# A fused attention, spectral-mixing and two-MLP kernel: folds, conversions and the loop's tail at other steps, batch 1's mixing on another engine

## The chip, the cores and the metric

The kernel runs on one core of a Trainium2 chip. The metric is the device time of one execution in microseconds (us); the time given for a kernel is the median of its runs. A core has TensorE (PE in the profile; PEld its weight loads), VectorE (DVE), ScalarE (ACT), GpSimd (POOL) and SyncE (SP, which here only starts DMA transfers). Each engine works through its own queue in order and waits there for what it needs from others.

## The reference

Three stages follow one another, in float32, for 2 batches of 768 tokens.

1. Clustered attention, 8 heads of dimension 64. Queries and keys are given to the nearest of 16 centroids (the largest product of normalised vectors); `scores = q k^T / 8`, and where the clusters of query and key differ, -1e9; softmax over the keys; times V. The heads side by side give x (768 x 512).
2. Mixing and MLP: `u = x + real(fft2(x))` over tokens and features; normalised over features; `u + relu(un @ w_ch1) @ w_ch2` with 2048 hidden features.
3. A second MLP with a gate: `h = relu(x @ w_in)` with 1024 hidden features, a convolution of width 3 over tokens, `(h * sigmoid(conv)) @ w_out`.

## The kernel before

Most products are made of three: each operand is split into a high part and a low part (what is left), and high x high, high x low and low x high are summed in PSUM (`pass3`, L84). So nearly every matrix is converted twice, by a copy with rounding (high) and by a subtraction (low).

**The attention loop** (L791) has one step for each of the 96 tiles of 128 queries (6 tiles for each of 16 heads), and its order is written out by hand under `manual_schedule`. Step n issues the first scores and the row maximum of tile n+8 (`score_max`, L552: four matmuls, then a VectorE reduction), the second scores of tile n with the maximum subtracted in the product (`score_exp`, L595: four matmuls, then `exp` on ScalarE), the high and low part of tile n-1's probabilities (`prob_hi`, L614, on ScalarE, for the last even tiles on VectorE; `prob_lo`, L623, on GpSimd, or on VectorE for the tiles in LO_ON_DVE), and the value products of tile n-3 (`attn_v`, L633: 18 matmuls; LAG is 3). First and second scores take turns in three PSUM slots with all else that `slot` gives out, so a slot comes free when the reduction or the `exp` of three slots ago is done. Tiles 89, 91, 93 and 95 (IN_PLACE) keep their probabilities in the PSUM slot until the low part is made.

All other work is hung on steps in lists: `pre` ahead of a step's own work, `mid` within it, `aft`, `post` and `fill` behind it, in this order (L663 to L762). For each pair of heads m this is its load, its cluster products (`prep_sims`, at step 12m-19, 24 matmuls), the one-hot masks, the split of queries and keys (`prep_hi`, `prep_lo`), and the scaling of V (`v_max`, `v_turn`, `v_step`). For batch 0 it is also the mixing (`mixing`, L95, with its plan at L702): `fold` adds and subtracts mirrored halves of x (GpSimd), "row" makes one row of an extra operand (three VectorE operations on one partition), "even" and "odd" combine the folds, `high_part` and `low_part` split them, and the products y, z, ab follow; then sums into U, and the normalisation (`norm`). Two weights of the first MLP are converted ahead, in four quarters at AHEAD_STEPS, and sent to memory until step 87.

**The first MLP** (L1014 to L1045) has 16 blocks of 128 hidden features for each batch. Here the tile framework's planner sets the order of each engine from the program's order and estimated times. Block f's up product (`mlp1_up`, L856: 24 matmuls, two results that ScalarE and VectorE turn into high and low parts) precedes block f-1's down product (`down`, L905: 18 matmuls). A weight arrives as 64-bit words; `load_w` (L312) loads one and turns it into float32 (`from64`: four VectorE operations, one on ScalarE), and `split_w` splits it. Batch 1's mixing runs beside batch 0's blocks as the generator `later` (L991), advanced twice in each down product; its folds, low parts and final adds are on GpSimd (`G` at L128, L146, L227, L235, L993).

Of the kernel before, what the change touches and what calls it, by code (L numbers as in the profile page):

```python
# [9 lines left out]
F16 = mybir.dt.float16  # L10
# [39 lines left out]
def tile_net(ctx, tc, qk, v, cen, w12, w34, conv, dft, odd, out):  # L50
# [44 lines left out]
    def mixing(b, bank, bank2, low, other):  # L95
# [50 lines left out]
        stage("odd0", -1, 0, G, "ov")(fold)  # L146
# [86 lines left out]
        def ab_mirror(j):  # L233
            xj = X[:, j + 3].rearrange("p (a n) -> p a n", a=2)[:, ::-1]
            G.tensor_add(xj, xj, d["m", j][:, N2 + 1:N2 + 515].rearrange("p (a n) -> p a n", n=257)[:, :, 0:256])  # L235
# [55 lines left out]
    wst, cvs, w32 = [], [], {}  # L291
# [20 lines left out]
    def load_w(k, f):  # L312
# [3 lines left out]
        for op in from64(w, raw):  # L316
            op()
# [27 lines left out]
    ws, hs, acc, xs, gps, wbp, ws_b = {}, {}, {}, {}, [], [], {}  # L345


    with ExitStack() as actx:
# [314 lines left out]
        for m in range(1, NH // 2):  # L663
            k = 12 * m - 24
            if m > 1:
                at(pre, k, load_raw, m)
                at(post, k + 5, prep_sims, m)
                at(fill, k + 6, prep_first, m)
                at(fill, k + 7, prep_pick, m)
                at(fill, k + 8, prep_hi, m, (0,))  # L670
                at(fill, k + 9, prep_lo, m, 0, G)
                at(fill, k + (9 if m < 7 else 8), prep_hi, m, (1,))
                at(mid, k + 11, prep_turn, m)
                at(fill, k + (10 if m < 7 else 9), prep_lo, m, 1, G)
            at(fill, k + 14, load_v, m)
            at(aft, k + 17, v_max, m)
            at(mid, k + 19, v_turn, m)
            for i in range(4):
                at(aft, k + 19, v_step, m, i)
            at(fill, k + 24, v_step, m, 4)  # L680
            at(fill, k + 25, v_step, m, 5)
# [7 lines left out]
        for h in range(NH):  # L689
# [4 lines left out]
            for i in range(3):  # L694
                at(fill, 6 * h + 8 + i, attn_out, h, i)

        def two(name):
# [3 lines left out]
        first = mixing(0, lambda name: slot(name)[:, 0], two, V, G)  # L701
        plan = (("even0", fill, 54), ("even1", fill, 55), ("row", aft, 57), ("even", fill, 58), ("evenH", aft, 59),  # L702
                ("evenL", fill, 59),
# [10 lines left out]
        for i, t in enumerate((0, 3, 1, 4, 2, 5)):  # L714
# [3 lines left out]
            at(aft, n + 2, scale, t)  # L718
# [40 lines left out]
        at(fill, 92, first_split, 0)  # L759
        at(fill, 93, first_split, 1)  # L760
        at(fill, 95, first_split, 2)
        at(fill, 97, first_split, 3)  # L762
# [28 lines left out]
        for n in range(-LEAD, 6 * NH + 10):  # L791
# [40 lines left out]
    identb = ident16.bitcast(BF16)  # L832
    V.tensor_copy(identb, ident)
# [22 lines left out]
    def mlp1_up(g, f):  # L856
        if (g, f) == (0, 0):
            h = hs[0, g, f] = [dp.tile([128, 780], F32R, tag=t, bufs=1, name=f"first{t}")[:, 0:S] for t in ("e0", "e1")]
            w = ws[0, g, f]
        else:  # L860
            if g:
# [267 lines left out]
```

## Time and profile before

| | |
|---|---|
| median of 3 runs | 701.85 us (699.71 to 702.35) |
| profiled execution, its own time | 702.69 us |
| its span, first to last instruction | 700.9 us |
| mean granted TensorE clock | 0.994 |
| TensorE busy | 667.3 us, 95% of the span |
| VectorE busy | 543.9 us, 78% |
| ScalarE busy | 410.8 us, 59% |
| GpSimd busy | 200.3 us, 29% |

All rows below come from the one profiled execution; times in them count from the start of its span. Idle time in brackets is that of the engine just ahead of the instruction, with what ended it. A group's row gives the name of the result, `<-`, and the names of the inputs.

### The profile page before, as it was taken

The numbers are of one execution on the slowest core, as the hardware profiler recorded it, in microseconds if no ns is written. First come the engines' busy times: TensorE is split into PE (matmuls) and PEld (weight loads), VectorE is DVE, ScalarE is ACT, GpSimd is POOL, SyncE is SP. The second block draws the span as 40 slices with busy tenths as digits, with TensorE's granted clock in tenths as the row PEclk, the third lists the DMA queues.
The fourth block names the chain that finished last, engine by engine and source line by source line (L and its number), as shares of the span: only waits on it lengthen the run. The fifth ranks groups of instructions, "written<-read, shape, count | busy, mean of one in ns | idle before, by whom it ended". The sixth has DMA issues, their size and how long they took to land.

```text
span 700.9 us, 12789 instructions
## 1 busy us (share of the span) xinstructions
PE 667.3 (95%) x5106; PEld 504.6 (72%) x5106; DVE 543.9 (78%) x873; ACT 410.8 (59%) x664; POOL 200.3 (29%) x168
## 2 busy tenths in 40 slices
PE   8799999998899997989999999999999999999997
PEld 6598988987799886869998998555555555555553
DVE  7777889898877997999469976997634399867662
ACT  3478869787458787536335654676534367555442
POOL 8156658568646945121041000000000000000000
PEclk9999999999899999999999999999999999999999
DMA  7747696773633413224203350243000000001002
GB/s 219 198 110 193 158 244 157 213 209 84 155 87 78 106 62 122 68 98 144 113 0 121 121 180 10 77 156 122 0 2 1 1 0 1 1 1 71 20 1 90
DMA packets 22087, 66.50 MB, mean 95 GB/s; under 512 B 4502, under 2 KB 7562, under 8 KB 19212
## 3 DMA queue, kind: packets, MB, share of 16 engines
q1 hardware_dynamic: 21020, 61.94, 31.0%
q0 software_dynamic: 1008, 3.75, 2.0%
q8 instruction: 40, 0.66, 0.4%
q14 instruction: 19, 0.16, 0.1%
HBM read 40.94 MB, written 5.77 MB: 67 GB/s over the span
## 4 chain that ended last, share of the span: by engine, by line
PE 72%; DVE 16%; DMA 4%; issue 2%; ACT 2%; POOL 2%; SPq 1%; DVEq 0%; ACTq 0%; POOLq 0%
PE acc L86 8%; PE acc L87 8%; PE acc L85 8%; PE up L85 5%; PE up L87 5%; PE up L86 5%; PE av L641 5%; PE s L566 3%; PE t L601 3%; PE s L568 3%; PE t L603 3%; DVE m L571 3%; PE sim L440 3%; PE u L85 2%; PE u L87 2%
## 5 line engine op out<-in xcount | busy, mean ns | idle before, releaser
L629 POOL TENSOR_TENSOR p<-p,p 128x768 f16<-128x768 f32 x62 | 107.5, 1735 | 85.7 <-ACT p L621 59.5
L571 DVE TENSOR_REDUCE m<-s 128x1 f32<-128x768 f32 x96 | 90.5, 947 | 13.8 <-PE s L568 6.5
L609 ACT ACTIVATE p<-t,cbias 128x768 f32<-128x768 f32 x92 | 82.8, 900 | 26.2 <-PE t L603 25.0
L621 ACT CAST p<-p 128x768 f16<-128x768 f32 x88 | 73.0, 830 | 1.2
L641 PE MATMUL av<-V,p 128*128 128x65 f16 x1728 | 70.8, 195 | 2.8 <-POOL p L629 2.8
L641 PEld LDWEIGHTS <-p 128*128 128x128 f16 x1728 | 59.3, 99 | 18.3 <-issue 15.1
L601 PE MATMUL t<-X 128*128 128x384 f32 x192 | 54.5, 365 | 8.6 <-DVE m L571 6.9
L566 PE MATMUL s<-X 128*128 128x384 f32 x192 | 56.2, 374 | 3.2 <-DMA X<-ohd 1.8
L568 PE MATMUL s<-Y 96*128 96x384 f32 x192 | 50.0, 341 | 1.1 <-DMA Y<-G 1.1
L603 PE MATMUL t<-Y 98*128 98x384 f32 x192 | 50.2, 343 | 0.0
L85 PE MATMUL up<-un,wha 128*128 128x384 f32 x120 | 41.3, 344 | 2.7 <-DVE YcL L163 1.3
L85 PE MATMUL u<-x,wb 128*128 128x384 f16 x128 | 41.7, 326 | 1.3 <-DVE h L892 0.9
L87 PE MATMUL up<-un,wla 128*128 128x384 f32 x120 | 40.5, 338 | 1.8 <-DVE wla L853 1.8
L601 PEld LDWEIGHTS t<-X 128*128 128x128 f32 x192 | 32.0, 192 | 13.9 <-issue 6.7
L85 PE MATMUL up<-un,wa 128*128 128x384 f16 x128 | 41.7, 326 | 0.0
L87 PE MATMUL up<-un,wa 128*128 128x384 f16 x128 | 41.7, 326 | 0.0
L86 PE MATMUL up<-un,wa 128*128 128x384 f16 x128 | 41.7, 326 | 0.0
L87 PE MATMUL u<-x,wb 128*128 128x384 f16 x128 | 41.7, 326 | 0.0
L86 PE MATMUL u<-x,wb 128*128 128x384 f16 x128 | 41.7, 326 | 0.0
L86 PE MATMUL up<-un,wha 128*128 128x384 f32 x120 | 40.5, 338 | 0.0
L629 DVE TENSOR_TENSOR p<-p,p 128x768 f16<-128x768 f32 x30 | 37.7, 1257 | 0.1
L85 PE MATMUL acc<-wb,gH 128*128 128x512 f16 x96 | 36.4, 379 | 0.5 <-ACT gH L900 0.5
(368 smaller groups left out, 1701.0 us busy)
## 6 DMA issues: line engine op xcount, KB each, us to landing
rawa<-w SPq DMA_DIRECT2D x14, 1024.0 KB
rawb<-w SPq DMA_DIRECT2D x8, 1024.0 KB
raw<-qk SPq DMA_DIRECT2D x7, 768.0 KB
X<-G SPq DMA_DIRECT2D x14, 384.0 KB
Y<-G SPq DMA_DIRECT2D x14, 384.0 KB
vraw<-v SPq DMA_DIRECT2D x8, 384.0 KB
out<-y SPq DMA_DIRECT2D x12, 256.0 KB
X<-G SPq DMA_DIRECT2D x14, 192.0 KB
```

Of the source, the lines that this page charges most:

```text
L85: T.matmul(o, sH, mH, start=start, stop=False)
L86: T.matmul(o, sH, mL, start=False, stop=False)
L87: T.matmul(o, sL, mH, start=False, stop=stop)
L566: T.matmul(t[:, c, 0:384], X[:, 0, sl], X[:, 1, 384 * c:384 * c + 384], start=True, stop=False)
L568: T.matmul(t[:, c, 0:384], Y[0:96, 0, sl], Y[0:96, 1, 384 * c:384 * c + 384], start=False, stop=True)
L571: V.tensor_reduce(m6s[h][:, i:i + 1], t[:, :, 0:384], AX.XY, ALU.max, negate=True)
L601: T.matmul(t[:, c, 0:384], X[:, 1, sl], X[:, 0, 384 * c:384 * c + 384], start=True, stop=False)
L603: T.matmul(t[:, c, 0:384], Y[0:98, 1, sl], Y[0:98, 0, 384 * c:384 * c + 384], start=False, stop=True)
L609: A.activation(p, t[:, :, 0:384], AF.Exp, bias=cbias, scale=0.125)
L621: A.copy(p16[:, 0], p32s[n])
L629: eng.tensor_sub(p16[:, 1], p, p16[:, 0])
L641: T.matmul(o, p16[:, k, 128 * j:128 * j + 128], v16[:, i, h % 2, 65 * part:65 * part + 65], start=(i + j + k + part == 0), stop=(i == 5), ...
```

## The change

- The two even folds of batch 0 go from steps 54 and 55 to 52 and 53. "row" is now computed from one fold alone, as -2 times its first row, in one ScalarE operation (aft of step 60 instead of 57) and one VectorE operation ("rowL", fill of step 60); the constant it is multiplied with is changed to match.
- `prep_first` of pair 6 goes to VectorE, both `prep_lo` of pair 7 too. V's steps for pairs 6 and 7 come earlier; the four small ones of the other pairs are spread over four steps. The last quarter of the weights converted ahead goes from steps 53 to 62 to steps 65 to 68. LO_ON_DVE names other tiles from 54 on: 12 instead of 13 up to tile 87, and 91 and 94.
- From tile 88 the value products lag four steps, with five buffers instead of four; the loop has one step more. Tile 91 is not converted in place, and tile 88's high part is made by ScalarE.
- Weight 0 is split earlier, weight 1 is split within the loop (`second_split`), and block 0's up product is issued in steps 96 and 97 (`first_up`). The squares of weights 0 and 1 go behind blocks 13 and 14.
- In the first MLP `load_w` splits the weight at once, its operations stay behind those of the load before it (`issue_after`), and from block 4 on weight f+2 instead of f+3 is loaded behind block f. The scales come one block later. Batch 1's mixing uses VectorE instead of GpSimd throughout.
- The bf16 identity is made on GpSimd at step 84 instead of VectorE.

```diff
-             | {n for n in range(54, 87) if n % 12 in (1, 2, 7, 11)} | {87})
+             | {54, 56, 59, 61, 62, 67, 73, 77, 80, 83, 86, 87, 91, 94})
-AHEAD_STEPS = [12 * q + n for q in range(1, 5) for n in (5, 5, 5, 12, 14)]
-IN_PLACE = range(89, 96, 2)
+AHEAD_STEPS = [12 * q + n for q in range(1, 4) for n in (5, 5, 5, 12, 14)] + [65, 65, 65, 67, 68]
+IN_PLACE = (89, 93, 95)
...
-        stage("even0", 1, 0, G, "ev")(fold)
+        stage("even0", 1, 0, rest, "ev")(fold)
...
-            r1 = dp.tile([1, N2], F32, tag="row", bufs=1, name=f"r1{b}")
-            ev = d["ev", 0], d["ev", 1]
-            V.tensor_sub(r1[:, 0:257], ev[0][0:1, 0, 0:257], ev[1][0:1, 0, 0:257])
-            V.tensor_copy(Zx[0:1, 0:257], r1[:, 0:257])
-            V.tensor_sub(Zx[32:33, 0:257], r1[:, 0:257], f32(Zx[0:1, 0:257]))
+            A.activation(Zx[0:1, 0:257], d["ev", 1][0:1, 0, 0:257], AF.Copy, scale=-2.0)
+
+        @stage("rowL")
+        def _():
+            V.scalar_tensor_tensor(Zx[32:33, 0:257], d["ev", 1][0:1, 0, 0:257], -2.0, f32(Zx[0:1, 0:257]), ALU.mult,
+                                   ALU.subtract)
...
-            G.tensor_add(xj, xj, d["m", j][:, N2:N2 + 518].rearrange("p (a n) -> p a n", n=259)[:, :, 0:256])
+            rest.tensor_add(xj, xj, d["m", j][:, N2:N2 + 518].rearrange("p (a n) -> p a n", n=259)[:, :, 0:256])
...
+    A_LOADS = [(3,), (4,), (5,), ()] + [(f + 2,) for f in range(4, 14)] + [()] * 2
...
-        for op in from64(w, raw):
-            op()
+        with tc.issue_after(last_op[0]) if last_op else nullcontext():
+            for op in from64(w, raw):
+                i = op()
+            last_op[:] = [i.ins]
+        if k == "a":
+            ws[0, 0, f] = split_w(hp, 3, "a", f, f"a{f}", V)
...
-            p16 = probs[n] = ap.tile([128, 2, S], F16, tag="p16", bufs=4, name=f"p16_{n}")
+            p16 = probs[n] = ap.tile([128, 2, S], F16, tag="p16", bufs=5, name=f"p16_{n}")
-            elif n > 87:
+            elif n > 89 and n % 2 == 0:
...
+                at(fill, k + 6, prep_first, m, V if m == 6 else G)
+                at(fill, k + 9, prep_lo, m, 0, G if m < 7 else V)
...
+            n = {6: (62, 64, 66, 67, 68), 7: (68, 71, 72, 74, 74)}.get(m, (k + 14, k + 17, k + 19, k + 24, k + 25))
+            at(fill, n[0], load_v, m)
+            at(aft, n[1], v_max, m)
+            at(mid, n[2], v_turn, m)
             for i in range(4):
-                at(aft, k + 19, v_step, m, i)
+                at(aft, n[2] + (i if m < 6 else i // 2), v_step, m, i)
...
-        plan = (("even0", fill, 54), ("even1", fill, 55), ("row", aft, 57), ("even", fill, 58), ("evenH", aft, 59),
+        plan = (("even0", fill, 52), ("even1", fill, 53), ("row", aft, 60), ("even", fill, 58), ("rowL", fill, 60),
...
+        def first_up(i):
+            if i == 0:
+                hs[0, 0, 0] = [dp.tile([128, 780], F32R, tag=t, bufs=1, name=f"first{t}")[:, 0:S] for t in ("e0", "e1")]
+            h, tk = hs[0, 0, 0], slice(384 * i, 384 * i + 384)
+            o = slot(f"up0_{i}")[:, 0, 0:384]
+            up_half(o, ws[0, 0, 0], uns[0], i)
+            A.activation(h[0][:, tk], o, AF.Relu)
+            V.scalar_tensor_tensor(h[1][:, tk], o, 0.0, f32(h[0][:, tk]), ALU.max, ALU.subtract)
...
+        at(post, 96, second_split, 0)
+        at(post, 96, first_up, 0)
+        at(post, 97, second_split, 1)
+        at(post, 97, first_up, 1)
...
-            if 0 <= n - LAG < 6 * NH:
+            if 0 <= n - LAG < 88:
                 attn_v(n - LAG)
+            elif 88 <= n - LAG - 1 < 6 * NH:
+                attn_v(n - LAG - 1)
...
-        for name, f in mixing(1, up_bank, lambda name: (up_bank(name + "b"), up_bank(name + "a")), G, V).items():
+        for name, f in mixing(1, up_bank, lambda name: (up_bank(name + "b"), up_bank(name + "a")), V, V, V).items():
...
-            down(0, g, f, side, (1, 4) if g == 0 else (2,))
-            if g == 0 and f + 3 < 16:
-                load_w("a", f + 3)
+            down(0, g, f, side, (1, 4) if g == 0 and f else (2,))
+            for i in A_LOADS[f] if g == 0 else ():
+                load_w("a", i)
...
-            if (g, f) == (0, 13):
+            if (g, f) == (0, 14):
                 scales("a")
...
-    cs[0] = (k1[0] % 2 == 0)
+    cs[0] = 1.0
```

## Rows read from the trace of the kernel before

**Rows 1.** By stretch: start:end, length, busy PE PEld DVE ACT POOL, clock, DMA, GB/s.

```profile
164.00:186.20 22.20, 16.79 (x184) 14.70 (x182) 19.58 (x25) 13.87 (x21) 18.82 (x15) 0.85 0.33 71
186.20:262.00 75.80, 74.30 (x828) 68.38 (x825) 64.94 (x110) 55.48 (x81) 47.22 (x33) 1.00 0.38 95
262.00:280.30 18.30, 14.11 (x240) 12.34 (x240) 13.12 (x26) 13.54 (x23) 8.82 (x6) 1.00 0.31 117
280.30:312.50 32.20, 28.13 (x148) 25.30 (x145) 31.28 (x38) 15.40 (x29) 7.11 (x7) 1.00 0.19 66
312.50:440.00 127.50, 126.82 (x669) 113.44 (x668) 99.44 (x140) 63.39 (x120) 15.95 (x14) 1.00 0.30 106
```

**Rows 2.** The same table, the stretch behind the longest wait.

```profile
178.20:184.10 5.90, 5.90 (x48) 5.28 (x49) 4.64 (x6) 2.83 (x4) 4.26 (x4) 0.52 0.73 159
```

**Rows 3.** Timeline (start, length, engine, line), steps 57 to 61.

```profile
169.29 0.94 DVE L571 TENSOR_REDUCE m<-s 128x1 f32<-128x768 f32 x1
...
171.37 1.85 DVE L135 TENSOR_TENSOR r<-ev,ev 1x257 f32<-1x257 f32 x1 [1.13 <-POOL ev L115]
...
175.06 1.74 DVE L137 TENSOR_TENSOR Zx<-r,Zx 1x257 fp32r<-1x257 f32 x1
...
178.18 0.98 PE L601 MATMUL t<-X 128*128 128x384 f32 x2 [5.34 <-DVE m L571]
...
184.91 0.52 PE L601 MATMUL t<-X 128*128 128x384 f32 x2
...
186.19 0.42 PE L85 MATMUL y<-DC,EH 128*128 128x386 f32 x1
```

**Rows 4.** Tile Zx: VectorE's operations, duration in ns (shortest/median/longest).

```profile
L136 DVE CAST Zx<-r x2: 283/1030/1776, 173.3 to 297.6; 1x257 fp32r<-1x257 f32 x2
L137 DVE TENSOR_TENSOR Zx<-r,Zx x2: 418/1080/1743, 175.1 to 298.8; 1x257 fp32r<-1x257 f32 x2
```

**Rows 5.** Timeline, PE's waits in the loop's tail.

```profile
268.74 0.67 PE L641 MATMUL av<-V,p 128*128 128x65 f16 x16 [1.23 <-POOL p L629]
...
272.68 0.58 PE L601 MATMUL t<-X 128*128 128x384 f32 x2 [1.18 <-DVE d L649]
...
279.22 1.23 PE L641 MATMUL av<-V,p 128*128 128x65 f16 x34 [1.59 <-POOL p L629]
```

**Rows 6.** First MLP: timeline, groups (count, busy us, mean ns), one down product's ends.

```profile
303.32 2.39 DVE L300 SCALAR_TENSOR_TENSOR wa<-rawa,wa 128x1024 int32<-128x1024 int32 x1
...
306.91 0.45 PE L87 MATMUL up<-un,wla 128*128 128x384 f32 x1 [1.75 <-DVE wla L853]
...
L853 DVE TENSOR_TENSOR wla<-wa,wha 128x1024 fp32r<-128x1024 f32 x15 | 18.8, 1250 | 6.6 <-ACT wha L851 6.6
L300 DVE SCALAR_TENSOR_TENSOR wa<-rawa,wa 128x1024 int32<-128x1024 int32 x14 | 18.2, 1303 | 0.2
...
404.14 0.40 PE L85 MATMUL acc<-wha,hH 128*128 128x512 f32 x1
...
408.24 0.34 PE L85 MATMUL up<-un,wha 128*128 128x384 f32 x1
```

**Rows 7.** Prices: a group of the page, tiles and lines (ns), timeline.

```profile
L571 DVE TENSOR_REDUCE m<-s 128x1 f32<-128x768 f32 x96 | 90.5, 947 | 13.8 <-PE s L568 6.5
...
L629 POOL TENSOR_TENSOR p<-p,p x62: 1642/1657/2492, 29.5 to 277.4; 128x768 f16<-128x768 f32 x62
L629 DVE TENSOR_TENSOR p<-p,p x30: 935/952/1981, 33.2 to 263.3; 128x768 f16<-128x768 f32 x30
L497 DVE TENSOR_TENSOR G<-raw,G x1: 959/959/959, 6.9 to 6.9; 128x768 fp32r<-128x768 f32 x1
L206 ACT COPY a<-a384p x2: 365/365/365, 213.2 to 340.6; 1x258 f32<-1x258 f32 x2
...
176.93 0.24 DVE L578 TENSOR_TENSOR mr<-s,mr 6x128 fp32r<-6x128 f32 x1
177.96 0.59 DVE L654 SCALAR_TENSOR_TENSOR U<-av,vsc,d 128x384 f32<-128x384 f32 x1
```

More of the change, by code (lines that the diff above doesn't have):

```diff
@@ L1 @@
 import numpy as np
-from contextlib import ExitStack
+from contextlib import ExitStack, nullcontext
 import concourse.bass as bass
@@ L93, in tile_net, with mixing @@
     YcH, YcL = (dp.tile([128, 2, 512], F32R, name=n) for n in ("YcH", "YcL"))
-    def mixing(b, bank, bank2, low, other):
+    def mixing(b, bank, bank2, low, other, rest):
         X = U[:, 6 * b:6 * b + 6, :]
@@ L145, in mixing @@
         stage("evenL", "ev", 257, "E", low)(low_part)
-        stage("odd0", -1, 0, G, "ov")(fold)
+        stage("odd0", -1, 0, rest, "ov")(fold)
         stage("odd1", -1, 1, other, "ov")(fold)
@@ L234, in ab_mirror @@
             xj = X[:, j + 3].rearrange("p (a n) -> p a n", a=2)[:, ::-1]
-            G.tensor_add(xj, xj, d["m", j][:, N2 + 1:N2 + 515].rearrange("p (a n) -> p a n", n=257)[:, :, 0:256])
+            rest.tensor_add(xj, xj, d["m", j][:, N2 + 1:N2 + 515].rearrange("p (a n) -> p a n", n=257)[:, :, 0:256])
         for j in range(3):
@@ L699, in two @@
             return t[:, 0], t[:, 1]
-        first = mixing(0, lambda name: slot(name)[:, 0], two, V, G)
-        plan = (("even0", fill, 54), ("even1", fill, 55), ("row", aft, 57), ("even", fill, 58), ("evenH", aft, 59),
-                ("evenL", fill, 59),
+        first = mixing(0, lambda name: slot(name)[:, 0], two, V, G, G)
+        plan = (("even0", fill, 52), ("even1", fill, 53), ("row", aft, 60), ("even", fill, 58), ("rowL", fill, 60),
+                ("evenH", aft, 59), ("evenL", fill, 59),
                 ("odd0", fill, 60), ("y0", post, 61), ("odd1", fill, 61), ("y0L", pre, 62), ("y1", post, 62),
@@ L757, in first_split, with second_split @@
                 V.tensor_copy(w[i], src)
[L759 to L762, printed above, removed]
+        def first_up(i):
[6 more added lines that the diff above has]
+            V.scalar_tensor_tensor(h[1][:, tk], o, 0.0, f32(h[0][:, tk]), ALU.max, ALU.subtract)
+        def second_split(i):
+            w = [t.rearrange("p a n -> p (a n)") for t in (YcH, YcL)]
+            if i:
+                V.tensor_sub(w[1], w32["a", 1], f32(w[0]))
+                ws[0, 0, 1] = [t[:, 512 * j:512 * j + 512] for j in range(2) for t in w]
+            else:
+                A.copy(w[0], w32["a", 1])
+        at(fill, 84, G.tensor_copy, identb, ident)
+        at(fill, 91, first_split, 0)
+        at(fill, 92, first_split, 1)
+        at(fill, 93, first_split, 2)
+        at(fill, 94, first_split, 3)
+        at(post, 96, second_split, 0)
+        at(post, 96, first_up, 0)
+        at(post, 97, second_split, 1)
+        at(post, 97, first_up, 1)
         prep_hi(0)
@@ L790, in tile_net @@
         parts[2] = stack_parts(2)
-        for n in range(-LEAD, 6 * NH + 10):
+        for n in range(-LEAD, 6 * NH + 11):
             for f in pre.get(n, []):
@@ L856, in mlp1_up @@
     def mlp1_up(g, f):
[L857 to L867 removed]
+        if g:
+            t = hp.tile([128, S], F32R, tag="hH", bufs=3, name=f"h{g}_{f}").bitcast(F16)
+            h = hs[0, g, f] = [t[:, 0:S], t[:, S:2 * S]]
+            w = ws[0, g, f] = split_16(hp, "a", f) if f == 0 else ws[0, g, f]
+        else:
+            h = hs[0, g, f] = [hp.tile([128, S], F32R, tag=t, bufs=3, name=f"{t}{g}_{f}") for t in ("hH", "hL")]
+            w = ws[0, g, f]
         for i in range(2):
@@ L1014, in tile_net @@
     side = later()
-    mlp1_up(0, 0)
-    for f in range(2):
-        squares("a", f, cvs[0].tile([128, 2048], I32, tag="raw64", bufs=2, name=f"junk{f}")[:, 0:256].bitcast(BF16))
     load_w("a", 2)
@@ L1024, in tile_net @@
                 next(side, None)
-            down(0, g, f, side, (1, 4) if g == 0 else (2,))
-            if g == 0 and f + 3 < 16:
-                load_w("a", f + 3)
+            down(0, g, f, side, (1, 4) if g == 0 and f else (2,))
+            for i in A_LOADS[f] if g == 0 else ():
+                load_w("a", i)
+            if g == 0 and f in (13, 14):
+                raw = cvs[0].tile([128, 2048], I32, tag="raw64", bufs=2, name=f"junk{f}")
+                squares("a", f - 13, raw[:, 0:256].bitcast(BF16))
             if g == 1 and f in B_LOADS:
                 load_w("b", B_LOADS.index(f))
-            if (g, f) == (0, 13):
+            if (g, f) == (0, 14):
                 scales("a")
```

26 lines of the change are left out of this document (7 added, 19 removed).

## The prediction

> **What bounds the kernel now.** I began with a table of busy time by stretch, because every engine works on something different in each stage. TensorE is the bound nearly everywhere, so the question is where it stands still. Subtracting its busy time from the length of each stretch [rows 1] leaves 5.4 us in 164 to 186 us (steps 54 to 60 of the attention loop), 1.5 us in 186 to 262, 4.2 us in 262 to 280 (the tail of the loop, steps 88 to 98), 4.1 us in 280 to 312 (the first blocks of the first MLP), and 0.7 us from there to 440. What lies before 164 us and behind 440 us is hardly touched. In the first of these stretches the clock is a second loss: right behind the wait, 5.9 us run at a granted clock of 0.52, the lower of the two levels, 1.2 GHz [rows 2], in which 2.8 us of work are lost. So the first stretch can give 8.2 us, the four others 10.5 us.
>
> The timeline of the first stretch [rows 3] shows why. VectorE works on "row", three operations on one partition and 257 elements. Each takes 1.74 to 1.85 us, while GpSimd, busy 18.8 of 22.2 us [rows 1], is at work beside it. The row maximum of the next tile stands behind them in VectorE's queue; its scores hold a PSUM slot, and TensorE waits 5.34 us for it. The same operations in batch 1 [rows 4] take 0.283 and 0.418 us with GpSimd quiet: the work is some 1.1 us, the rest is waiting for GpSimd. The tail [rows 5] has three waits: 1.23 and 1.59 us for low parts of probabilities that come late from GpSimd, and 1.18 us that the list puts down to a small VectorE operation. There the slot of tile 91, which is converted in place in PSUM, is the likelier cause. In the MLP's first blocks [rows 6], TensorE waits 1.75 us for a weight's low part, which stood behind a 2.39 us weight conversion that normally takes 1.2 to 1.3.
>
> **Part by part.**
>
> *Folds and row.* The two even folds go from steps 54 and 55 to 52 and 53, where the cluster products (24 matmuls behind step 53) leave all other engines time. GpSimd finds a gap there, and its queue is then: low part 51, fold, low part 52, fold, low part 53. The first fold needs head 7's output, which precedes it in the same step. Low part 53 is due at step 56, with two of 1.66 [rows 7] and one fold ahead of it in the queue from step 53 on. The row's three VectorE operations become one on ScalarE (nearest row: 0.365 us for a copy of 258 elements on one partition) and one on VectorE (0.418 alone, 1.743 beside GpSimd [rows 4, 7]). Behind it in VectorE's queue now stands only step 61's maximum, and VectorE has slack from there, since the three y products (ten matmuls each) keep TensorE busy. The odd fold must wait for this operation, as both use one buffer; its first product is four steps away.
>
> What is late next is VectorE itself. From the maximum of tile 65 (start 169.3 [rows 3]; prep_first comes ahead of it, but low part 55 leaves, so I keep the start) to the end of that of tile 68, which releases the scores of step 61, it has four maxima of 0.95; low part 56, the even sum and its low part at 0.95 each (the last by the nearest row, 128x768, 0.959); one head output of 0.59; and seven small ones at 0.2 (nearest row 0.24) [rows 7]. This is 3.8 + 2.85 + 0.6 + 1.4 = 8.7 us. To it comes waiting for GpSimd. A low part on VectorE takes 0.952 in the median and 1.981 at worst [rows 7], so the three large ones add between 0 and 3.1; I take the middle, 1.5, because GpSimd, now busy 18.8 of 22.2 us [rows 1], is left with gaps. The end is 169.3 + 10.2 = 179.5, and the first y product 1.3 later, the distance from the scores of step 61 to it (184.91 to 186.19 [rows 3]): 180.8 instead of 186.2. That is a gain of 5.4 us; bounds: 3.8 with every wait, 8.2 with TensorE as the only limit. The slow clock is within it.
>
> Here a rule speaks against the change. Rows first: beside GpSimd the same operation is 1.3 to 1.5 us longer on VectorE, whatever its size [rows 4], and an operation that reads PSUM stays at 0.59 [rows 7]. The Trainium skill, "SBUF — State Buffer", section "SBUF: two separate sides", calls it an exclusive lock: a VectorE operation with two SBUF inputs and a GpSimd operation block each other for a whole instruction. By that rule each operation moved from GpSimd to VectorE exposes itself to such a wait, and the gain would be the lower bound, 3.8. The rows agree on the mechanism, and their median says that it does not hit each time.
>
> *The other operations at other steps.* The last quarter of the early weight conversion leaves steps 53, 60 and 62 for 65 to 68, four VectorE operations, with its load and store on SP's queue; the second cluster products and the first z product stand there. The last head pair's low parts (two of 0.959 alone, up to 2 beside GpSimd) go to VectorE at step 69, two fewer low parts of probabilities are on it later, and V's conversion for the last two pairs comes 5 to 11 steps earlier, with its load two or three steps ahead of its first use (three now). Cover: in 186 to 262 us VectorE is busy 64.9 of 75.8 [rows 1]. With this cover gone the price would be the two low parts, 2 us. V's conversion and two low parts leave steps 72 to 77, where the queue is full; I take a gain of 0.7 of the 1.5 us of waits, bounds -2 and 1.5. The spread of V's four small operations for the earlier pairs only splits a block: nothing, 0 to 0.5.
>
> *Tail.* From tile 88 the value products lag one step more, with a fifth buffer for probabilities; tile 91 leaves PSUM at once; low part 94 goes from GpSimd (1.66) to VectorE (0.95) [rows 7]; the squares of the first two weights leave ScalarE; and the first up product of the MLP (24 matmuls) is put between the last value products, so that it fills what waits are left. TensorE's work is unchanged. VectorE, busy 13.1 of 18.3 us there [rows 1], gets low part 94 (0.95), the second weight's low part (1.25 [rows 6]) and two low parts of the up product, and loses one high part: some 3 us more in a shorter time, which only just fits. Of 4.2 us I take 3.6, bounds 1.5 and 4.2.
>
> *First MLP.* Batch 1's folds, low parts and adds go to VectorE, ten operations, four of 0.96 [rows 7] and six shorter, under 10 us spread over 80, and its waits for GpSimd go: 1.2 us at the 2.39 row alone [rows 6]. The low part of a weight now precedes the next weight's conversion. But TensorE arrives 3.6 us earlier with the same conversions ahead, so the first blocks still wait for VectorE: of 4.1 us I take 1.5 as gained, bounds -3 and 4.1. The scales one block later: 0 to 4, taken as nothing, because the last down product is independent of them and covers their chain. The ones without a path (the bf16 identity on GpSimd, the constant's first row): 0.
>
> **Sum.** 5.4 + 0.7 + 3.6 + 1.5 = 11.2 us off the profiled execution's 702.69 (span 700.9, 1.8 around it): 691.5. That execution is 0.84 above the median of the three runs, 701.85, so carried to the median it is 690.6.
>
> **Rivals.**
> 1. *VectorE is the next wait in steps 54 to 60.* For it: it is busy 19.6 of 22.2 us there [rows 1], and it takes prep_first and low parts 54 and 56. Against it: 5.4 us of its busy time are the row. Then the first part gives 3.8 and the second -2: sum 3.8 - 2 + 3.6 + 1.5 = 6.9, time 695.
> 2. *The tail's gain is given back at once.* VectorE is busy 31.3 of 32.2 us in the first blocks [rows 1]; if TensorE only arrives earlier, the fourth part is -3 instead of 1.5: sum 5.4 + 0.7 + 3.6 - 3 = 6.7, time 695. Against it: the waits for GpSimd that go.
> 3. *Slower: each weight arrives too late.* From block 6 on a weight's load stands in the program directly ahead of its up product, one block later than now. If its conversion is not taken ahead, five operations of about 1.2 us [rows 6], 6 us, must fit under one down product of 4.1 us (404.14 to 408.24 [rows 6]): 1.9 us of wait in each of ten blocks, 19 us. The gains without the first blocks are 9.7, so the time is 711; it decides from five such blocks on. Against it: now the order is the program's only in part, and conversions start well before the down product ahead of them has ended.
> 4. *The change does not relieve GpSimd*, because the folds merely delay low parts 52 and 53: then TensorE waits at steps 55 and 56, and with tail and rest unchanged the gain is 3 us or less: 699.
>
> **How the numbers follow.** Forecast 0.64, rivals 1 and 2 0.13 and 0.13, rival 3 0.06, rival 4 0.04. A measurement of this kernel can tell about 0.5%, 3.5 us, from no change. The forecast and 0.22 of rivals 1 and 2 are faster than that (0.86), the 0.04 of them that goes worse and rival 4 lie within it (0.08), rival 3 beyond on the other side (0.06). The range: low with the first part at its ceiling and two more near theirs (8.2 + 1.2 + 4.2 + 4.0 = 17.6, off the median 701.85), 684; high with rivals 1 and 2 together (3.8 - 2 + 3.6 - 3 = 2.4, 699.5), cut to what leaves one in ten outside, 698.5.
>
> **What would show it.** In the changed profile TensorE's longest wait on a row maximum between steps 54 and 61 is under 2 us, the granted clock stays at 1.00 there (2.4 GHz), the two row operations take under 0.5 us on ScalarE and under 1.8 on VectorE, the wait for GpSimd's low parts in the tail is gone with up matmuls in its place, and the blocks behind have under 3 us of waits for VectorE. Wrong would be: waits for weight low parts block after block (rival 3), a wait for VectorE of 3 us or more in the first blocks (2), or a stall at half clock at steps 56 to 60 again (1, 4).

## The result, and the profile after

The changed kernel takes 692.25 us (median of 4 runs, 689.78 to 693.6); the kernel before, measured beside it, 701.89. The ratio is 0.9857 (95% interval 0.983 to 0.9883), a gain of 9.6 us; 690.6 was forecast. The profiled execution is the shortest of the four, 689.78 with a span of 688.0, so in its rows 12.9 us are gone.

The busy times of the page come first, then the table by stretch, which answers to [rows 1] and has its columns. The first stretch begins 1.7 us earlier than there, as the steps ahead of it do; the next two are cut at the first y product and at step 88; the tail now holds the first up product, so that it ends at the second weight's.

```profile
PE 664.9 (97%) x5106; PEld 503.0 (73%) x5106; DVE 546.1 (79%) x883; ACT 413.8 (60%) x667; POOL 179.9 (26%) x153
...
162.30:178.79 16.49, 14.81 (x183) 12.30 (x182) 15.23 (x21) 13.79 (x22) 11.91 (x8) 1.00 0.30 68
178.79:256.50 77.71, 74.82 (x830) 68.69 (x826) 69.37 (x114) 55.65 (x81) 48.46 (x35) 1.00 0.49 132
256.50:276.78 20.28, 18.31 (x268) 16.25 (x264) 18.58 (x30) 14.69 (x21) 7.28 (x5) 1.00 0.01 2
276.78:308.00 31.22, 31.22 (x160) 28.85 (x161) 30.91 (x44) 16.43 (x30) 0.00 (x0) 1.00 0.28 98
308.00:440.00 132.00, 131.68 (x703) 113.83 (x702) 106.15 (x167) 69.99 (x135) 7.11 (x7) 1.00 0.26 90
```

TensorE still bounds the kernel. Its idle time in steps 54 to 60 falls from 5.4 to 1.7 us and the clock there rises from 0.85 to 1.00 (2.4 GHz); in the first MLP's blocks it falls from 4.1 to nothing. In the long stretch between, it grows, from 1.5 to 2.9.

The same landmarks in both traces give where the 12.9 us lie. Up to step 53 the trace is 1.7 us shorter (the head of the kernel, not touched). From there to the first y product 5.7 are gained, from it to step 88 1.9 given back. The tail, up to where TensorE is free for the second weight's up product, gains 2.4. The first MLP up to the second MLP's first product gains 4.4; the 0.8 us that TensorE waited for VectorE ahead of the second weight's up product, before the change, are counted here. All behind it gains 0.6.

The timeline of steps 57 to 61, answering [rows 3]:

```profile
167.85 0.94 DVE L578 TENSOR_REDUCE m<-s 128x1 f32<-128x768 f32 x1
...
176.41 0.95 DVE L578 TENSOR_REDUCE m<-s 128x1 f32<-128x768 f32 x1
176.92 0.40 ACT L133 ACTIVATE Zx<-ev 1x257 fp32r<-1x257 f32 x1
...
177.42 0.62 PE L608 MATMUL t<-X 128*128 128x384 f32 x2 [0.19 <-DVE m L578]
...
178.00 2.52 POOL L118 TENSOR_TENSOR ov<-U 128x765 f32<-128x765 f32 x1
178.79 0.42 PE L85 MATMUL y<-DC,EH 128*128 128x386 f32 x1
178.85 1.96 DVE L137 SCALAR_TENSOR_TENSOR Zx<-ev,Zx 1x257 fp32r<-1x257 f32 x1
...
180.84 0.96 DVE L578 TENSOR_REDUCE m<-s 128x1 f32<-128x768 f32 x1
180.86 0.44 PE L155 MATMUL y<-OD,Zx 128*128 128x386 f32 x1 [0.23 <-DVE Zx L137]
...
181.85 0.62 PE L573 MATMUL s<-X 128*128 128x384 f32 x2 [0.55 <-DVE m L578]
```

From the maximum of tile 65 to the end of that of tile 68 VectorE takes 9.5 us (167.85 to 177.36), where 10.2 were predicted and 14.1 were taken before (169.29 to 183.38). The row's low part still meets a GpSimd fold and takes 1.96 us. Two waits of TensorE follow from it: 0.23 us of the last matmul of the first y product (L155), and 0.55 us of the next first scores, whose slot is held until the maximum behind the row's low part (180.84) is done.

Three of TensorE's waits from the list of waits (total, times, longest), and the timelines of the two longer ones:

```profile
PE t L608 <- DVE m L578: 1.9, 7, 0.4
...
PE unT L275 <- DVE p L634: 1.8, 1, 1.8
PE s L573 <- DVE m L223: 1.2, 1, 1.2
...
209.85 1.66 POOL L636 TENSOR_TENSOR p<-p,p 128x768 f16<-128x768 f32 x1 [6.06 <-ACT p L628]
209.99 2.35 DVE L506 TENSOR_TENSOR G<-raw,G 128x768 fp32r<-128x768 f32 x1
...
214.08 0.58 PE L573 MATMUL s<-X 128*128 128x384 f32 x2 [1.25 <-DVE m L223]
...
261.02 1.65 POOL L636 TENSOR_TENSOR p<-p,p 128x768 f16<-128x768 f32 x1
261.08 1.87 DVE L270 TENSOR_SCALAR y<-U,mv,rs 128x512 f32<-128x512 f32 x1
...
262.87 0.94 DVE L634 TENSOR_TENSOR p<-t,p 128x768 f16<-128x768 f32 x1
263.87 0.66 PE L275 MATMUL unT<-ident,y 128*128 128x128 f32 x4 [1.84 <-DVE p L634]
...
270.51 0.42 PE L85 MATMUL up<-un,firstEH 128*128 128x384 f32 x1
```

At step 69 a low part of pair 7, now on VectorE, is held by GpSimd and takes 2.35 us; the eviction of the mixing's products (L223), for which TensorE waits, stands behind it. The wait itself falls in step 71. In the tail the last normalisation of batch 0 is held in the same way (1.87 us; 0.54 where nothing holds it). The changed kernel issues it ahead of its step's own work instead of behind it, a move that the list of the change does not name. Tile 89's low part now stands behind it, and the transposed U waits for the slot of that tile. The up product (from 270.51) fills what waits followed.

### The profile page after: what moved, and what is told of

It is laid out like the page before. It is cut to its first block, busy times and chain, and to the rows that moved or that the text cites. A ratio compares the mean times of both kernels' runs of the same rounds, so it can differ in the third digit from the quotient of the medians.

```text
span 688.0 us, 12771 instructions
## 1 busy us (share of the span) xinstructions
PE 664.9 (97%) x5106; PEld 503.0 (73%) x5106; DVE 546.1 (79%) x883; ACT 413.8 (60%) x667; POOL 179.9 (26%) x153
## 4 chain that ended last, share of the span: by engine, by line
PE 68%; DVE 20%; ACT 3%; issue 3%; DMA 2%; POOL 1%; SPq 1%; DVEq 0%; POOLq 0%
PE acc L87 7%; PE acc L85 7%; PE acc L86 7%; PE up L85 5%; PE up L86 5%; PE up L87 5%; PE av L648 4%; PE s L573 3%; DVE m L578 3%; PE t L608 3%; PE s L575 3%; PE sim L447 3%; PE t L610 3%; PE u L85 2%; PE u L87 2%
## 5 line engine op out<-in xcount | busy, mean ns | idle before, releaser
L628 ACT CAST p<-p 128x768 f16<-128x768 f32 x90 | 74.7, 830 | 1.3
L636 DVE TENSOR_TENSOR p<-p,p 128x768 f16<-128x768 f32 x31 | 39.2, 1265 | 0.2
L85 PE MATMUL up<-un,wha 128*128 128x384 f32 x112 | 38.0, 339 | 0.0
L86 PE MATMUL up<-un,wha 128*128 128x384 f32 x112 | 37.8, 338 | 0.0
L87 PE MATMUL up<-un,wla 128*128 128x384 f32 x112 | 37.6, 337 | 0.0
```

The lines of the kernel that those rows point to most:

```text
L85: T.matmul(o, sH, mH, start=start, stop=False)
L86: T.matmul(o, sH, mL, start=False, stop=False)
L87: T.matmul(o, sL, mH, start=False, stop=stop)
L636: eng.tensor_sub(p16[:, 1], p, p16[:, 0])
```

## The experiments

Twelve kernels in three groups. Each group has its own runs of the kernel before: medians 703.32, 702.75 and 701.44 us for groups one to three; ratios are to these.

**Group one: the row alone.** The kernel before with

```diff
-            ("row", aft, 57), ("even", fill, 58)
+            ("row", aft, 60), ("even", fill, 58), ("rowL", fill, 60)
```

with the new "row" and "rowL" and the constant's first row.

> The kernel before with the row alone changed: one ScalarE operation in the aft list of step 60 and one VectorE operation in the fill list, with the constant's first row; the folds stay at steps 54 and 55. Theory (the stall is three VectorE operations that each wait for a GpSimd instruction): the 5.3 us wait of TensorE at step 59 and the half clock behind it go, the first y product comes 4 to 7 us earlier, and the time falls by 4 to 7 us, ratio 0.990 to 0.994. Rival (the stall is GpSimd's lateness, because the folds stand in its queue between the low parts): TensorE still waits 3 us or more between steps 55 and 61 and the ratio is above 0.996.

Measured: 701.7 us, ratio 0.9983 (0.9958 to 1.0008), no difference clear of the noise. Its table by stretch and one row of its timeline:

```profile
160.00:180.00 20.00, 16.22 (x195) 13.83 (x195) 17.14 (x23) 15.56 (x23) 20.00 (x16) 1.00 0.32 71
...
300.00:320.00 20.00, 16.63 (x74) 15.29 (x73) 17.23 (x20) 10.14 (x19) 1.89 (x2) 0.83 0.29 105
...
179.91 1.06 PE L642 MATMUL av<-V,p 128*128 128x65 f16 x16 [2.10 <-POOL p L630]
```

The wait for VectorE is gone; GpSimd is busy all of the 20 us, and TensorE waits for its low parts. Yet this trace is 4.3 us ahead of the one before at the first up product's eviction (278.39 against 282.68; 2.0 of them lie ahead of step 46, where the kernels are the same), and only 1.6 at the end. The rest is lost in the first MLP. TensorE's waits there add up to 4.0 us in both traces; what differs is the clock behind them, 0.83 between 300 and 320 us instead of 1.00.

**The folds alone.** The kernel before with

```diff
-            ("even0", fill, 54), ("even1", fill, 55)
+            ("even0", fill, 52), ("even1", fill, 53)
```

> The kernel before with the two even folds alone at steps 52 and 53; the row stays three VectorE operations at step 57. Theory: the row no longer waits for the fold (1.1 us), but its three operations still meet a busy GpSimd, so they take 1 to 1.8 us each, TensorE still waits 2 us or more for the row maximum, and the gain is 0 to 2.5 us, ratio 0.9965 to 1.000. Rival (GpSimd's lateness is the cause): the stall is gone, ratio 0.994 or less.

Measured: 700.84 us, ratio 0.9972 (0.9948 to 0.9996). The theory holds: the row's stall remains, the longest wait for a maximum is 2.9 us, and the gain of 2.5 us is at the upper end of its range.

**The changed kernel once more**, as the base of the others.

> The changed kernel as it is, once more, beside the partial ones. Median 691 to 693.5 us, ratio 0.983 to 0.988. If an execution with a mean granted clock near 0.995 is recorded, the stretch in which the clock is low should lie directly behind a wait of TensorE, and tell what the difference of some 3 us between its executions is.

Measured: 690.8 us (690.04 to 693.85), ratio 0.9834 (0.9794 to 0.9875). The profiled execution (692.44 us) has the same waits, but behind the one of 1.84 us its clock is 0.91 between 260 and 280 us.

**Batch 1's mixing back on GpSimd.** The changed kernel with

```diff
-        for name, f in mixing(1, up_bank, ..., V, V, V).items():
+        for name, f in mixing(1, up_bank, ..., G, V, G).items():
```

> The changed kernel with batch 1's first folds, low parts and final adds on GpSimd again (the other folds on VectorE, as before the change). Theory (the first blocks' waits came from VectorE operations held up by GpSimd): VectorE's conversions near the folds take over 2 us again and TensorE loses 1.5 to 3 us in the first blocks of the first MLP, 1.5 to 3 us slower than the changed kernel. Rival (the order of the conversions, with the low part ahead of the next weight, did it): TensorE has no wait in the first blocks and the time is within 1 us of the changed kernel.

Measured: 698.56 us, ratio 0.9944 (0.9922 to 0.9966): 7.8 us slower than the changed kernel, far more than either theory had. Timeline and table of its first blocks:

```profile
289.79 2.82 POOL L115 TENSOR_TENSOR ev<-U 128x765 f32<-128x765 f32 x1
290.83 1.80 DVE L113 TENSOR_TENSOR ev<-U 128x3 f32<-128x3 f32 x1
...
306.95 0.45 PE L85 MATMUL y<-DC,EH 128*128 128x386 f32 x1 [3.65 <-DVE hL L900]
...
300.00:320.00 20.00, 16.36 (x78) 14.89 (x77) 17.56 (x19) 10.47 (x19) 2.98 (x3) 0.91 0.33 114
```

A VectorE operation on three columns takes 1.80 us beside GpSimd's fold (0.15 in the changed kernel); a low part of the hidden features comes 3.65 us late, and the clock falls behind it.

**Group two: folds and row together**, in the kernel before (both diffs above).

> The kernel before with the two even folds at steps 52 and 53 and, together with it, the new row (one ScalarE operation and one VectorE operation at step 60); GpSimd's list of low parts, the tail and the first MLP stay as before. Folds alone gave 2.5 us and the row alone 1.6 us, each with a wait of 2 to 3 us left in steps 54 to 61. Theory (two limits stand side by side, VectorE's row and GpSimd's queue, and only both together free TensorE): the gain is more than the sum of the two, 5 to 8 us, about 696 us; no wait over 1.5 us between 160 and 185 us, the clock 1.00 there, and the first y product at about 179 to 181 us instead of 186.2. Rival (the relief of GpSimd from low parts 54, 56, 59 is needed as well): 3 to 4 us, 699 to 700 us, with a wait of 2 us or more for a low part of GpSimd left in steps 55 to 62.

Measured: 703.65 us, ratio 1.0018 (0.9994 to 1.0042). The theory of two limits falls, and so does the rival: there is no wait for GpSimd there. Timeline and table:

```profile
180.57 2.32 DVE L303 SCALAR_TENSOR_TENSOR ahead<-ahead 128x512 uint32<-128x512 uint32 x1
...
182.92 1.74 DVE L137 SCALAR_TENSOR_TENSOR Zx<-ev,Zx 1x257 fp32r<-1x257 f32 x1
...
184.72 0.44 PE L155 MATMUL y<-OD,Zx 128*128 128x386 f32 x1 [2.24 <-DVE Zx L137]
...
180.00:200.00 20.00, 17.21 (x162) 15.70 (x161) 17.10 (x21) 10.00 (x15) 8.51 (x6) 0.91 0.40 110
```

The first y product starts at 180.62, as forecast. Its last matmul waits 2.24 us for the row's low part, which stands in VectorE's queue behind a step of the early weight conversion (L303, step 60), itself held by GpSimd. The clock falls behind this wait.

**The mixing off GpSimd alone.** The kernel before with batch 1's `G, V` turned into VectorE throughout (folds and final adds through the new argument `rest`).

> The kernel before with one thing changed: batch 1's folds, low parts and final adds on VectorE instead of GpSimd. In the changed kernel putting them back on GpSimd cost 7.8 us. Theory (the gain of the first MLP is this move alone): TensorE's waits for VectorE behind 300 us shrink from 4.1 us to under 1.5, gain 3 to 5 us, 697 to 699 us. Rival (the move pays only together with the first up product in the loop and the weights' new order, because VectorE, 31.3 of 32.2 us busy there, has no room for ten more operations): 0 to 1.5 us, or slower by up to 3.

Measured: 697.53 us, ratio 0.9924 (0.9898 to 0.995), 5.2 us faster. The theory holds. Its first blocks, answering to the fourth line of [rows 1], and three groups of VectorE between 280 and 312 us, first before, then here:

```profile
280.00:312.00 32.00, 31.25 (x162) 28.72 (x161) 31.47 (x45) 16.52 (x30) 0.00 (x0) 1.00 0.27 99
...
L300 DVE SCALAR_TENSOR_TENSOR wa<-rawa,wa 128x1024 int32<-128x1024 int32 x4 | 6.0, 1510 | 0.0
L299 DVE TENSOR_SCALAR wa<-rawa 128x1024 int32<-128x1024 int32 x4 | 4.3, 1106 | 0.0
L115 DVE TENSOR_TENSOR ev<-U 128x765 f32<-128x765 f32 x1 | 2.6, 2612 | 0.0
...
L300 DVE SCALAR_TENSOR_TENSOR wa<-rawa,wa 128x1024 int32<-128x1024 int32 x4 | 4.9, 1215 | 0.0
L299 DVE TENSOR_SCALAR wa<-rawa 128x1024 int32<-128x1024 int32 x4 | 2.7, 684 | 0.0
L115 DVE TENSOR_TENSOR ev<-U 128x765 f32<-128x765 f32 x2 | 1.9, 954 | 0.0
```

VectorE is about as busy as before (30.8 us of these 32 then), with 45 operations instead of 37. The same operations are shorter now: by the three groups some 4.5 us of its busy time before were waiting for GpSimd (4 times 0.30, 4 times 0.42, and 1.66), and that is where the moved operations found room.

**The normalisation back in its place.** The changed kernel with

```diff
-            at(aft if t != 5 else pre, n + 2, scale, t)
+            at(aft, n + 2, scale, t)
```

> The changed kernel with the last normalisation of batch 0 (scale of tile 5) back behind low part 89 in VectorE's order, as before the change. Theory (its two VectorE operations stand ahead of tile 89's low part, one of them held 1.3 us by GpSimd, and so the slot of tile 89 in PSUM comes free 1.8 us late for the transposed U of the MLP): the wait of 1.84 us at that product falls under 0.8 us, and so does the half clock that stood behind it in one of two profiles; 1 to 2.5 us faster than the changed kernel, 689 to 690 us. Rival (the transposed U then waits for its normalised input instead, as scale comes later): within 0.5 us, 690.5 to 691.5 us, or slower.

Measured: 691.51 us, ratio 0.9835 (0.9811 to 0.9859): no difference, as the rival said. The transposed U waits 1.1 us for its normalised input instead of 1.8 for the slot.

**The first up product back at the MLP's start**, in the changed kernel:

```diff
-        at(post, 96, first_up, 0)
-        at(post, 97, first_up, 1)
...
+    mlp1_up(0, 0)
     load_w("a", 2)
```

> The changed kernel with the first up product (24 matmuls of the two halves, 2 evictions and 2 low parts) taken out of the tail and put back at the start of the MLP. Theory (in the tail it fills TensorE's waits, worth most of the 2.4 us that the tail gained): waits of 1 to 1.6 us for probabilities' low parts and the last value products return, 1.5 to 3 us slower than the changed kernel, 692.5 to 694 us. Rival (the waits went through the longer lag and low part 94 on VectorE, and the place of the up product does nothing): within 0.7 us of the changed kernel.

Measured: 694.81 us, ratio 0.989 (0.9869 to 0.9912), 3.3 us slower than the run above it and 4.0 slower than the changed kernel of group one: at least as much as the whole tail had gained hangs on this place; the longer lag without it shows no gain in this trace. The waits that the theory named do not come back, though: the longest two for low parts or value products there are 0.7 and 0.3 us. What it has beside the wait of 1.8 us for tile 89's slot is one of 1.1 us for VectorE at the second weight's up product, and a clock of 0.91 between 260 and 280 us.

**Group three: four parts together.** The kernel before with folds, row, batch 1's mixing on VectorE, and

```diff
-             | {n for n in range(54, 87) if n % 12 in (1, 2, 7, 11)} | {87})
+             | {54, 56, 59, 61, 62} | {n for n in range(63, 87) if n % 12 in (1, 2, 7, 11)} | {87})
```

> The kernel before with four parts of the change together: the even folds at steps 52 and 53, the new row, the low parts of tiles 54, 56, 59, 61 and 62 on VectorE (before: 55, 59, 61, 62; so GpSimd loses 54 and 56 and gets 55), and batch 1's mixing on VectorE. The last of these alone gave 5.2 us (697.5); row and folds together gave nothing by themselves, with 2.2 us of wait left for the row's low part and two of 1.6 for GpSimd. Theory (GpSimd's list of low parts was what still held steps 52 to 61, and what those steps give was given back in the first blocks of the MLP as long as batch 1's mixing was on GpSimd): now 4 to 5 us more than with the mixing alone, 692.5 to 694 us, no wait over 1.5 us in steps 54 to 61. Rival 1 (the weight conversion that stands at steps 60 and 62 takes the place of the wait): 1 to 2 us more than the mixing alone, 695.5 to 697 us. Rival 2 (the list of low parts does nothing): 697 to 698 us.

Measured: 697.98 us, ratio 0.994 (0.9916 to 0.9964). Rival 2: no more than the mixing alone. The wait at L155 is still there, 2.27 us, with the clock at 0.83 between 180 and 200 us.

**The same with the last weight conversion at steps 65 to 68:**

```diff
-AHEAD_STEPS = [12 * q + n for q in range(1, 5) for n in (5, 5, 5, 12, 14)]
+AHEAD_STEPS = [12 * q + n for q in range(1, 4) for n in (5, 5, 5, 12, 14)] + [65, 65, 65, 67, 68]
```

> The same as the run above it in this list, and besides that the last quarter of the early weight conversion at steps 65 to 68 instead of 53, 60 and 62, as in the changed kernel. Theory (steps 54 to 61 are free by then): within 0.7 us of the run above. Rival (VectorE's conversion at steps 60 and 62 is the next wait): 2 to 4 us faster than the run above, 691 to 693 us. What still differs from the changed kernel is then the tail, the first up product, the weights' order and V's parts; by the run with the up product put back these are worth 2 to 4 us in the changed kernel.

Measured: 693.92 us (690.87 to 699.09), ratio 0.9897 (0.9861 to 0.9932). The runs scatter, and the two intervals overlap by 0.0016; the medians are 4.1 us apart, close to the 2 to 4 of the rival. The trace is clearer: the row's low part is as long as ever, and the conversion no longer stands ahead of it.

```profile
180.89 1.94 DVE L137 SCALAR_TENSOR_TENSOR Zx<-ev,Zx 1x257 fp32r<-1x257 f32 x1
...
182.88 0.44 PE L155 MATMUL y<-OD,Zx 128*128 128x386 f32 x1 [0.19 <-DVE Zx L137]
```

The distances between three landmarks of each trace, in us, settle these steps. They start from the exponential of tile 46 (141.97 us in the trace before), so that what differs ahead of it drops out, and end with that of tile 62:

| kernel | tile 46 to first y | first y to tile 62 | sum |
|---|---|---|---|
| before | 44.2 | 3.5 | 47.7 |
| mixing off GpSimd (steps 46 to 62 unchanged) | 43.2 | 3.5 | 46.7 |
| row | 40.8 | 4.6 | 45.4 |
| folds | 43.3 | 3.5 | 46.8 |
| folds, row | 38.7 | 7.8 | 46.4 |
| folds, row, low parts, mixing | 39.4 | 8.1 | 47.4 |
| the same with the conversion moved | 38.6 | 4.7 | 43.3 |
| changed kernel | 38.3 | 4.8 | 43.0 |

The second line shows what two executions of the same steps can differ by, 1 us. Folds and row give the 5.5 us up to the first y product; without the conversion's move 4.3 of them are lost again by step 62.

**Weights one block earlier**, in the changed kernel:

```diff
-    A_LOADS = [(3,), (4,), (5,), ()] + [(f + 2,) for f in range(4, 14)] + [()] * 2
+    A_LOADS = [(3,), (4,), (5,), (6,), (7,), (8,), ()] + [(f + 2,) for f in range(7, 14)] + [()] * 2
```

> The changed kernel with the weights of the first MLP loaded and converted one block earlier from block 3 on, as the order before had it, so that no weight stands directly ahead of its up product. The prediction's rival 3 held that the late place costs 1.9 us in each of ten blocks. Theory (the profile of the changed kernel shows no wait of TensorE there, so the place is free): within 0.7 us of the changed kernel, 690 to 691.5 us. Rival (the earlier place crowds VectorE in blocks 3 to 8, where it is 19.8 of 20 us busy): waits for low parts of 1 us and more there, 1.5 to 4 us slower.

Measured: 691.41 us, ratio 0.986 (0.9832 to 0.9887): no difference. The edit moves three weights (6 to 8), whose place is free; the seven behind them and the order itself (each weight split directly behind its conversion) were not undone. In the changed kernel's trace no up product of batch 0's blocks waits for a weight.

**Two moves undone**: the normalisation as above, and pair 7's low parts on GpSimd.

```diff
-                at(fill, k + 9, prep_lo, m, 0, G if m < 7 else V)
+                at(fill, k + 9, prep_lo, m, 0, G)
```

> The changed kernel with two of its moves undone: the last head pair's two low parts back on GpSimd (on VectorE one of them took 2.35 us beside a GpSimd low part, and TensorE waited 1.25 us at step 69), and the last normalisation of batch 0 back behind low part 89 (alone: no difference). Theory (the moved low parts are why steps 61 to 88 gave back 1.9 us): the wait of 1.25 us is gone, 0.7 to 1.5 us faster than the changed kernel, 689.3 to 690.1 us. Rival (GpSimd's low parts of probabilities are then late instead, each low part taking it 2.5 us): waits for GpSimd of 1 us or more in steps 69 to 73, within 0.7 us of the changed kernel or up to 2 us slower.

Measured: 693.03 us, ratio 0.9881 (0.9857 to 0.9905), 1.6 us slower than the run above it by the medians; the two intervals overlap. The wait of 1.25 us is gone, and another has come:

```profile
223.22 1.65 POOL L636 TENSOR_TENSOR p<-p,p 128x768 f16<-128x768 f32 x1
...
223.82 4.18 DVE L636 TENSOR_TENSOR p<-p,p 128x768 f16<-128x768 f32 x1
...
224.83 1.08 POOL L228 TENSOR_TENSOR U<-U,m 128x512 f32<-128x512 f32 x1
...
225.88 1.28 POOL L236 TENSOR_TENSOR U<-U,m 128x512 f32<-128x512 f32 x1
...
227.12 1.32 POOL L265 TENSOR_TENSOR rs<-rs,half 128x1 f32<-128x1 f32 x1
...
231.71 0.98 PE L573 MATMUL s<-X 128*128 128x384 f32 x2 [3.94 <-issue]
```

Four GpSimd operations run one behind the other, and a VectorE low part of 0.95 us [rows 7] takes 4.18. V's step and the eviction of the mixing's products stand behind it in VectorE's queue, and TensorE stands for 3.94 us; that it waits for this eviction is inferred, since the list names no releaser here. No version tried beats the changed kernel.

The later stretches of the same traces, in us, from the exponentials of tiles 62 and 88, the second weight's up product and the second MLP's first product:

| kernel | tile 62 to 88 | 88 to second up product | from there to the second MLP |
|---|---|---|---|
| before | 73.5 | 22.3 | 279.8 |
| row | 73.6 | 22.4 | 282.1 |
| folds, row | 74.1 | 22.4 | 281.3 |
| mixing off GpSimd | 73.5 | 22.3 | 276.4 |
| folds, row, low parts, mixing | 74.9 | 22.4 | 274.3 |
| the same with the conversion moved | 73.5 | 22.4 | 274.4 |
| changed kernel | 74.2 | 19.0 | 276.2 |
| changed kernel once more | 74.3 | 20.2 | 276.3 |
| first up product back | 74.5 | 22.5 | 276.3 |
| two moves undone | 76.8 | 18.1 | 276.3 |

The 0.8 us of wait ahead of the second weight's up product are in the middle column here. Two things stand out. With pair 7's low parts on GpSimd steps 62 to 88 take 2.5 us more. And in the first MLP the changed kernel is no faster than the mixing alone, and 1.9 us slower than the two kernels with the new row and the weights' old order. TensorE has no wait over 0.15 us there in those two traces and three in the changed one, 1.3 us in all; the first, 0.3 us, is for ScalarE's scaling of a weight for batch 1's blocks, which needs the scales that now come later. Which edit costs the rest was not tried.

## Why the prediction was right, and where it was not

The total, 690.6 against 692.25 and 690.8 in two groups of runs, came out of terms that were off in both directions: by the trace 0.3 too little, 2.6 and 1.2 too much, and 2.9 too little. That they add up to nearly the forecast is luck. What was right is the mechanism of the larger parts: TensorE's waits came from VectorE and GpSimd delaying each other, and they went with the operations that were moved.

**Folds and row** (predicted 5.4, measured 5.7 to the first y product). The queue of VectorE was counted rightly: 9.5 us for 10.2. The step that failed is the sentence that behind the row's low part "stands only step 61's maximum, and VectorE has slack from there". VectorE had no slack there: the row's low part, held by GpSimd, makes the maximum behind it 0.55 us late for TensorE. And the sentence asked what stands behind the row's low part and not what stands ahead of it: the weight conversion of step 60. I had priced that operation's move with "the other operations", as near nothing; with folds, row, low parts and mixing in place it is worth 4.1 us (47.4 to 43.3 in the table). Whether folds and row would still be needed with the conversion moved alone was not tried. "The slow clock is within it" held: 1.00 there. The row's operations took 0.40 us on ScalarE, under the 0.5 I named, and 1.96 on VectorE, over the 1.8, at the cost of the two waits of 0.23 and 0.55 us. Low parts 54 and 56 on VectorE show no gain of their own.

By the exclusive lock (the Trainium skill, "SBUF — State Buffer", section "SBUF: two separate sides") the first part was to give 3.8, with each of three large VectorE operations held. The rows agree that such waits come (1.96 us beside a fold of 2.52), but not each time: the three took 1.26, 1.65 and 0.97 us, 1.0 more than alone, where I took 1.5 and the bound 3.1. That the delay is 1.3 to 1.5 us "whatever its size" was read from operations of one size; in the runs the delay varies, from 0.02 and 0.70 us for two of these three to 1.4 for the 128x768 at 209.99 and 1.65 for the three columns.

**Steps 61 to 88** (predicted 0.7 gained, measured 1.9 given back; rival 1 had -2 here). Of it 1.3 lie between the first y product and tile 62, the rest behind it, with the wait of 1.25 us in step 71 that pair 7's low parts cause. I had named their price, 2 us without cover, and taken the cover for granted. Leaving them on GpSimd is no better: by the trace of the last run these steps are then 2.5 us longer, though by its times the difference is not clear of the noise.

**The tail** (predicted 3.6, measured 2.4). The right mechanism, mis-sized: the two waits for GpSimd are gone, but there is a new one of 1.84 us behind the moved normalisation, which the sum did not have. Moving it back leaves one of 1.1 us. The up product in the loop is by itself worth about what I gave the whole tail: taking it out costs 3.3 to 4.0 us.

**The first MLP** (predicted 1.5, measured 4.4). The step that failed is "TensorE arrives 3.6 us earlier with the same conversions ahead, so the first blocks still wait for VectorE". I read VectorE's 31.3 of 32.2 us as work. Some 4.5 us of it were waiting for GpSimd: with 44 operations instead of 38 its busy time is 30.9 of 31.2, and TensorE waits no longer. (GpSimd gave up 13 operations in all; the prediction's ten leave out three small ones of the folds.) The move is worth 5.2 us alone and 7.8 within the change; by the last table it is nearly all that the first MLP gained. The term of the scales, taken as nothing, is a wait of 0.3 us. Rival 2, the gain given back at once, did not come, and the run with the row alone does not show it either: its waits in the first MLP are as long as before, and the 2.7 us lost there go with the lower clock.

**Rivals 3 and 4.** No weight comes too late: the later place of the weights costs nothing that the run with earlier loads could show. GpSimd was relieved: busy 11.9 of 16.5 us instead of 18.8 of 22.2.

The 1.7 us ahead of step 53 belong to no term. They are of the size by which executions differ (below), and the median, 2.5 us above the profiled execution, does not contain them for certain.

## What to carry to other kernels

Part of the time in which a profile shows an engine as busy may be waiting for another: compare the same operation's duration with and without that neighbour before you write that it has no room. Follow a moved operation to the very instruction that needs its result, and list what stands ahead of it in its queue as well as behind it. A part that shows no gain in the total may have one that is lost a little later: row and folds gained 5.5 us up to the first y product and lost 4.3 of them until the next operation in the queue was moved too.

## What the runs showed of the hardware

**The same wait of TensorE is followed by a lower clock in one execution and not in another.** In the kernel's head TensorE waits 2.1 us for `mh`. Two kernels that are the same there, the one with weights earlier first (timeline row, then the table by stretch):

```profile
21.82 2.19 PE L596 MATMUL first_max<-ident,mh 128*2 128x128 f32 x12 [2.12 <-DVE mh L593]
...
20.00:24.00 4.00, 2.17 (x13) 1.24 (x13) 1.61 (x4) 0.00 (x0) 0.00 (x0) 0.80 1.02 210
24.00:28.00 4.00, 3.47 (x18) 3.15 (x17) 2.33 (x4) 0.79 (x1) 0.00 (x0) 0.77 1.03 206
```

The one with two moves undone:

```profile
21.98 1.47 PE L596 MATMUL first_max<-ident,mh 128*2 128x128 f32 x12 [2.12 <-DVE mh L593]
...
20.00:24.00 4.00, 2.02 (x15) 1.58 (x16) 1.77 (x4) 0.51 (x1) 0.00 (x0) 1.00 0.97 210
24.00:28.00 4.00, 3.31 (x22) 2.98 (x21) 3.21 (x5) 1.26 (x4) 0.00 (x0) 1.00 0.99 202
```

Nine of the 14 profiles have a clock of 0.91 between 20 and 40 us, five have 1.00: 0.09 of 20 us is 1.8 us. What decides it stays open. The wait of 1.84 us in the tail goes the same two ways: 0.91 between 260 and 280 us in the changed kernel's second profile, 1.00 in its first. So the first profile, with the clock at 1.00 throughout, is 2.5 us under its own median, and a wait taken away is worth more than its length in some executions only.

**A VectorE operation can stand through several GpSimd operations, not one.** The 4.18 us above are the clearest row. The Trainium skill, "SBUF — State Buffer", section "SBUF: two separate sides", says that whichever of the two starts first has the shared ports for its whole instruction, and the other blocks. Here a low part that began beside one GpSimd operation ended 0.84 us behind the end of the third (225.88 + 1.28 = 227.16), which is about what it takes alone; that the ports went to GpSimd three times in a row is inferred from this. Operations with one SBUF input are longer beside GpSimd too: 1.87 us for the normalisation of the tail, 0.54 elsewhere in the same trace.
